# A gated mix of linear attention and a GLU: the first half's down products in seven-product form, weight sums in place, and PSUM tiles seeded from PSUM

## The chip, the cores and the metric

The kernel runs on one core of one Trainium2 chip. The metric is the device time of one execution in microseconds; the median of the runs is compared.

## The reference, cut to what matters

```python
x = A_x                                   # [1, 2048, 640], float32
g = sigmoid((x * gate_w).sum(-1, keepdims=True))
# A: linear attention, 32 heads of 20
q, k, v = heads(x @ A_wqkv)
pq, pk = phi(q), phi(k)                   # t + 1 where t > 0, else exp(t); plus 1e-6
kv, z = einsum("bhsd,bhse->bhde", pk, v), pk.sum(over s)
a = merge(einsum("bhqd,bhde->bhqe", pq, kv) / (einsum("bhqd,bhd->bhq", pq, z) + 1e-6)) @ A_wo
# B: GLU, F = 1536
b = (sigmoid(x @ B_w_gate) * (x @ B_w_up)) @ B_w_down
return g * a + (1 - g) * b
```

## The kernel before

**Numbers and products.** Every float32 operand of a matmul is split into a high half in TensorE's fp32r type and a low half that holds the rest (`split`: a ScalarE copy makes the high half, a VectorE subtraction the low one). One product is then three matmuls, high x high, high x low and low x high (`mm3`, lines 229 to 232), which accumulate in one PSUM tile. `prod` strings several products together. PSUM has eight tiles of 128 x 512, two each under the tags ch, dd, cc and rot, and `ps_tile` takes the two of a tag in turn.

**Fewer products.** Where a 2 x 2 block of weight tiles meets a 2 x 2 block of input tiles, the kernel takes Winograd's form with seven products in place of eight. It needs sums of the weight blocks (S1 to S4) and of the input blocks (T1 to T4), all split again. In the code B11, B12, B21 and B22 are the four input blocks, A11, A12, A22 weight blocks.

**Stages.** The tokens are worked in two halves of 1024 (groups 2 and 3 first, called `pr` = 1, then groups 0 and 1, `pr` = 0), each as two groups of 512 columns. First comes k and its product with x, for all tokens. Then for each half: q (`q_phase`), twelve blocks of 128 rows of F (`f_phase`), and the last down products (`last_down`). At the end the attention output is put together (`a_unit`, `ABlock`).

**One F block** has seven steps (class `Block`, `s1` to `s7`), 18 products, 54 matmuls. `s1` and `s2` are the gate's first tile of a group, in tiles ch and dd; their sum is made by a ScalarE copy of ch into an SBUF tile c11 and a VectorE add of dd. `s3`, `s5` and `s6` go on accumulating in ch, `s4` and `s7` in cc. Step 5 ends with a ScalarE copy and a VectorE add that give c22. The steps of neighbouring blocks interleave: s3, s4, s5 of block f, s1 and s2 of block f+1, then s6 and s7 of block f. Tails (`tail_f`, `tail_s`) make sigmoid(gate) x up, the h of the block, during the next block's steps 3 to 5.

**Weights.** In the first half each F block's gate and up weights come from memory as float32 (`load_w`), are split (`wg_split`, `u_part`), summed into a tile wsum (`sums`), and the sums are split into ws in two parts (`s_part`, needed at steps 3 and 5). All forms are also stored to scratch in memory, so that the second half loads them ready (`load_form`). The same is done with the down weights: `split_d` makes wd, `queue_ds` the sums and their forms ds.

**Down products.** They take h back to 640 rows and accumulate into the SBUF tile tb of 5 x 2 tiles (o = 0 to 4, groups 0 and 1). In the first half, `down_unit` makes them in the plain way: while block f runs, the pair of blocks before it gives five units of two products, for one of the two groups. In the second half `down_pair` makes both groups of a pair of blocks at once, in the seven-product form, spread over the steps of every odd block: V and W belong to o = 4, and X, Y and Z with a suffix 0 or 1 to the two column pairs o = 0, 1 and o = 2, 3. Each partial product is added into tb by VectorE (`add`), or copied by ScalarE where it is the first for its place. The last pair of each half is left to `last_down`.

**Order.** Nothing is scheduled by the compiler: instructions run on each engine in the order in which the Python code emits them. The class `Order` keeps an estimated clock for TensorE, ScalarE and VectorE (`a_cost`, `v_cost`). Side work (splits, sums, chains for the denominators) stands in queues, from urgent over items and lazy to chain and spare; `fill` emits an entry when its estimated end is at most 0.6 us (ScalarE) or 1.2 us (VectorE) past TensorE's clock, and `need(key)` emits what has not been emitted when a product is about to read it.

**Denominators.** `queue_den(g)` makes the factor of one group of 512 tokens: it loads five tiles of phi(q) again, multiplies them by z, sends the sums through memory to turn them, takes the reciprocal and sends it through memory again. Group 2's chain runs in the first half, group 3's in the q stage after it, groups 0 and 1 in the second half.

Of the kernel before, what the change touches and what calls it, by code (L numbers as in the profile page):

```python
# [29 lines left out]

class Order:

# [150 lines left out]

# [3 lines left out]

def v_cost(w):
    return 0.155 + w * 0.00104


@with_exitstack
def gated_mix_kernel(ctx: ExitStack, tc: tile.TileContext, xt, xn, wk, wv, wo, wst_q, wst_f, out_t):
# [16 lines left out]

    def ps_tile(tag):
        return psum.tile([P, 512], F32, name=tag, tag=tag, bufs=2)
# [10 lines left out]

# [35 lines left out]
    ones_f = common.tile([P, P], F32, name="ones_f")  # L274
# [19 lines left out]

# [10 lines left out]

# [6 lines left out]

# [5 lines left out]

# [8 lines left out]


# [29 lines left out]

# [10 lines left out]


# [102 lines left out]

# [28 lines left out]

# [3 lines left out]

# [48 lines left out]

# [4 lines left out]
    def queue_qw(u):  # L560
# [34 lines left out]
        for n, t in enumerate((a22, a11, a21, a12, g5)):  # L595
            piece(2, n * w, t)
# [44 lines left out]

# [71 lines left out]

# [96 lines left out]

# [28 lines left out]
    for k in range(2, KC):  # L839
        b1.k(k)  # L840
        if k == 2:
# [6 lines left out]

    nc.gpsimd.memset(logit[:, S // P:], 0.0)
    nc.gpsimd.memset(ones_f, 1.0)  # L850
    nc.gpsimd.affine_select(bd, ones_f[:bdn, :bdn].rearrange("p (b c) -> p b c", c=DH),
                            pattern=[[-DH, HPG], [0, DH]], base=0, channel_multiplier=1,
# [3 lines left out]

# [176 lines left out]

# [25 lines left out]

    entries = [("q", 1, 0)] + [("f", 1, f) for f in range(FC)]  # L1060
    WST, WS, W_AT = {}, {}, {}
# [30 lines left out]
    def queue_s(n, first=0, last=2):  # L1092

        def sums(part):
            g, u = WST[n][:, 0], WST[n][:, 1]
            if part == 0:
                WS[n] = pw2.tile([P, 9 * P], F32, name="wsum", tag="wsum")
            s = WS[n]
            c = [slice(2 * i * P, 2 * (i + 1) * P) for i in range(4)]
            if part == 0:  # L1100
                add(s[:, c[0]], u[:, c[0]], u[:, c[1]])
                sub(s[:, c[2]], g[:, c[0]], u[:, c[0]])
            else:
                sub(s[:, c[1]], s[:, c[0]], g[:, c[0]])
                sub(s[:, c[3]], g[:, c[1]], s[:, c[1]])
                sub(s[:, 8 * P:], g[:, 4 * P:], u[:, 4 * P:])
# [6 lines left out]
        cut = (0, 4 * P, 9 * P)  # L1113

        def s_part(part):
# [4 lines left out]
            split(h[:, cs], l[:, cs], WS[n][:, cs])  # L1120
# [4 lines left out]
        if first == 0:  # L1125
            order.add(0, 2 * v_cost(2 * P), lambda: sums(0), None, lambda: W_AT.get(n, 1e9))
            order.add(0, 3 * v_cost(2 * P), lambda: sums(1))
        if last > 1:
            order.add(a_cost(3 * P), v_cost(3 * P), u_part)
# [6 lines left out]
    class Block:  # L1136


        def __init__(self, n):
            self.n = n  # L1140
# [14 lines left out]
        def s1(self):  # L1155
            self.ch, self.c11 = ps_tile("ch"), c_tile("c11")
            prod(self.ch, [self.xa(0, j, j) for j in range(2)], True)
            act(self.c11, self.ch, AF.Copy, "p")

        def s2(self):  # L1160
            self.dd = ps_tile("dd")
            prod(self.dd, [self.xa(0, k, k) for k in range(2, KC)], True)
            add(self.c11, self.dd, self.c11, "p")

        def s3(self):
            self.c12 = c_tile("c12")
            prod(self.ch, self.xt(2, 2, 1), False)
            act(self.c12, self.ch, AF.Copy, "p")

        def s4(self):  # L1170
            self.cc = ps_tile("cc")
            prod(self.cc, self.xt(2, 0, 0) + [self.xb(1, 2, 4)], True)

        def s5(self):
            self.c22 = c_tile("c22")
            prod(self.ch, self.xt(2, 4, 2), False)
# [6 lines left out]
        def s7(self):  # L1183
            prod(self.cc, [self.xb(2, 6 + j, 2 + j) for j in range(2)] + [self.xb(2, 8, 4)], False)
            add(self.c12, self.cc, self.c12, "p")

# [33 lines left out]

    def gate_store():

        n = S // P
        t = tt("gates").rearrange("p (a n c) -> p a n c", n=2, c=H)
# [10 lines left out]


# [51 lines left out]

# [102 lines left out]

    down_pool, down_cms = [], []
    HT, DST, WD = {}, {}, {}
# [24 lines left out]

    def queue_ds(p):
        w, v = 4 * P, 2 * P
# [14 lines left out]
        def forms(j, h):  # L1437
            t = down_pool[1].tile([P, 2, v], F32R, name="ds", tag="ds", bufs=3)
            split(t[:, 0], t[:, 1], DST[("f", 1, 2 * p + j)][0][:, h * v:(h + 1) * v])

            def rest():
                c = 2 * D + j * w + h * v
                nc.gpsimd.dma_start(wd_dram[p][:, :, c:c + v], f32(t))
                if h:
                    load_d()
                if not (j or h):
# [907 lines left out]
```

## Time and profile before

| | |
|---|---|
| median of 3 runs | 737.26 us (737.07 to 737.29) |
| profiled execution, span from first to last instruction (the only time of it that is given) | 735.1 us |
| TensorE busy | 730.7 us, 99%, 3605 matmuls |
| VectorE busy | 554.3 us, 75%, 978 instructions |
| ScalarE busy | 334.2 us, 45%, 625 instructions |
| GpSimd busy | 97.6 us, 13%, 161 instructions |
| moved by DMA | 173.53 MB, mean 236 GB/s |

In the profile PE is TensorE's matmuls, PEld its weight loads, DVE is VectorE, ACT ScalarE, POOL GpSimd and SP the queue that issues most transfers. L230 to L232 are the three matmuls of a product, L242 any ScalarE activation, L246 any VectorE operation on two tensors, so groups are told apart by their tiles (out<-in). A time of an engine that is busy counts overlapping instructions once.

### The profile page before, as it was taken

Reading aid. Unit: us, or ns where it says so; the run is one execution under the profiler, and the core shown is the slowest. Engines: PE = TensorE matmul, PEld = TensorE weight load, DVE = VectorE, ACT = ScalarE, POOL = GpSimd, SP = SyncE. Lnnn points to the kernel's source line nnn. Section 1 sums busy time; section 2 is a strip of 40 time slices with the busy share of each in tenths; the row PEclk is TensorE's granted clock in tenths of the full one; section 3 lists DMA queues with packets and bytes.
Section 4 is the critical chain, followed back from the end, with each engine's and each line's share of the span. In section 5 each row is a group of like instructions: output and inputs, shape, how many; then the busy total and the mean of one; then the engine's idle time right before and its main releaser. Section 6 shows DMA issues by size and latency. Waiting matters only on the chain.

```text
span 735.1 us, 10117 instructions
## 1 busy us (share of the span) xinstructions
PE 730.7 (99%) x3605; PEld 628.8 (86%) x3605; DVE 554.3 (75%) x978; ACT 334.2 (45%) x625; POOL 97.6 (13%) x161
## 2 busy tenths in 40 slices
PE   9999999999999999999999999999999999999998
PEld 8999999988888888888888888888888888888886
DVE  5988877987776667877887864556778777779976
ACT  5764748268555634344444364344323222224541
POOL 0210111113312212112211211000000031000000
PEclk9999999999999999999999999999999999999999
DMA  8574648688887767666966668977778686659312
GB/s 262 134 204 99 181 115 269 162 292 304 310 319 265 290 218 274 239 237 222 365 253 224 257 206 314 352 227 249 262 264 306 253 229 242 217 200 345 113 70 100
DMA packets 70968, 173.53 MB, mean 236 GB/s; under 512 B 11610, under 2 KB 32362, under 8 KB 67206
## 3 DMA queue, kind: packets, MB, share of 16 engines
q1 hardware_dynamic: 54550, 109.99, 45.5%
q0 software_dynamic: 16224, 62.74, 24.1%
q8 instruction: 28, 0.46, 0.3%
q10 hardware_dynamic: 144, 0.16, 0.1%
q14 instruction: 22, 0.18, 0.1%
HBM read 103.96 MB, written 63.92 MB: 228 GB/s over the span
## 4 chain that ended last, share of the span: by engine, by line
PE 99%; DVE 0%; issue 0%
PE ch L230 10%; PE ch L231 10%; PE ch L232 10%; PE dd L231 8%; PE dd L230 8%; PE dd L232 8%; PE cc L232 7%; PE cc L231 7%; PE cc L230 7%; PE rot L231 6%; PE rot L232 6%; PE rot L230 6%; PE rot L1359 1%; PE rot L324 0%; PE ch L806 0%; PE dd L806 0%
## 5 line engine op out<-in xcount | busy, mean ns | idle before, releaser
L242 ACT ACTIVATE c<-ch 128x512 f32<-128x512 f32 x90 | 53.7, 597 | 184.0 <-PE ch L232 182.1
L246 DVE TENSOR_TENSOR hf<-c,hf 128x512 fp32r<-128x512 f32 x63 | 43.3, 689 | 38.8 <-ACT hf L242 38.7
L246 DVE TENSOR_TENSOR c<-cc,c 128x512 f32<-128x512 f32 x56 | 38.6, 690 | 33.8 <-ACT c L242 23.6
L246 DVE TENSOR_TENSOR tb<-dd,tb 128x512 f32<-128x512 f32 x73 | 49.7, 688 | 16.2 <-PE dd L232 16.0
L242 ACT ACTIVATE c<-c 128x512 f32<-128x512 f32 x60 | 37.8, 629 | 48.3 <-DVE c L246 47.9
L242 ACT ACTIVATE hf<-c 128x512 fp32r<-128x512 f32 x63 | 39.2, 624 | 17.1 <-DVE c L246 16.8
L246 DVE TENSOR_TENSOR tb<-rot,tb 128x512 f32<-128x512 f32 (+1 forms) x61 | 40.9, 679 | 5.2 <-PE rot L232 5.1
L230 PE MATMUL ch<-xth,ws 128*128 128x512 f32 x112 | 43.7, 390 | 0.0
L232 PE MATMUL ch<-xth,ws 128*128 128x512 f32 x112 | 43.6, 389 | 0.0
L231 PE MATMUL ch<-xtl,ws 128*128 128x512 f32 x112 | 43.6, 389 | 0.0
L230 PE MATMUL dd<-xrh,wg 128*128 128x512 f32 x90 | 35.1, 390 | 0.0
L232 PE MATMUL dd<-xrh,wg 128*128 128x512 f32 x90 | 35.0, 389 | 0.0
L231 PE MATMUL dd<-xrl,wg 128*128 128x512 f32 x90 | 35.0, 389 | 0.0
L230 PE MATMUL cc<-xbh,ws 128*128 128x512 f32 x84 | 32.7, 389 | 0.0
L231 PE MATMUL cc<-xbl,ws 128*128 128x512 f32 x84 | 32.7, 389 | 0.0
L232 PE MATMUL cc<-xbh,ws 128*128 128x512 f32 x84 | 32.7, 389 | 0.0
L231 PE MATMUL rot<-pkl,xnh 128*128 128x320 f32 x102 | 31.5, 309 | 0.0
L232 PE MATMUL rot<-pkh,xnl 128*128 128x320 f32 x102 | 31.4, 308 | 0.0
L230 PE MATMUL rot<-pkh,xnh 128*128 128x320 f32 x102 | 31.4, 308 | 0.0
L246 DVE TENSOR_TENSOR c<-c,c 128x512 f32<-128x512 f32 x44 | 30.2, 686 | 1.3 <-ACT c L242 0.9
L242 ACT ACTIVATE ws<-wsum 128x512 fp32r<-128x512 f32 (+1 forms) x26 | 17.5, 681 | 24.7 <-DVE wsum L246 24.3
L232 PEld LDWEIGHTS ch<-xth,ws 128*128 128x128 f32 x112 | 21.0, 188 | 4.4
(590 smaller groups left out, 2241.0 us busy)
## 6 DMA issues: line engine op xcount, KB each, us to landing
wf<-ws POOLq DMA_DIRECT2D x12, 1152.0 KB, 6.2
ws<-wf SPq DMA_DIRECT2D x12, 1152.0 KB, 7.6
wst<-wst_f SPq DMA_DIRECT2D x12, 640.0 KB, 5.5
wf<-wg POOLq DMA_DIRECT2D x12, 640.0 KB, 4.9
wd<-wd POOLq DMA_DIRECT2D x12, 640.0 KB, 5.8
wg<-wf SPq DMA_DIRECT2D x12, 640.0 KB, 6.0
xst<-xt SPq DMA_DIRECT2D x10, 640.0 KB, 6.8
wf<-wd SPq DMA_DIRECT2D x10, 640.0 KB, 5.6
```

The lines of the kernel that those rows point to most:

```text
L230: nc.tensor.matmul(out, l_hi, r_hi, start=first, stop=False, skip_group_check=True)
L231: nc.tensor.matmul(out, l_hi, r_lo, start=False, stop=False, skip_group_check=True)
L232: nc.tensor.matmul(out, l_lo, r_hi, start=False, stop=last, skip_group_check=True)
L242: nc.scalar.activation(out, src, fn, **kw)
L246: nc.vector.tensor_tensor(out, a, b, op=op)
L1359: nc.tensor.matmul(ps[:w, :w], v[:, m, :w], gt[:, m, c0:c0 + w], start=(m == 0), stop=(m == KC - 1))
```

## The change

Down products of the first half. `down_pair(pr, p)` now serves both halves. In the first half it reads the weights straight from wd and from ds, which is now one tile of eight column blocks, while they are also stored as before. The tails of the first half make T1 to T4 (`tail_s`), and h forms get four more buffers there. Inside `down_pair`, the first products W, X0 and X1 are no longer added into tb by themselves: ScalarE copies them into a second PSUM tile (`seed`), where V, Y0 and Y1 go on accumulating. `ps_borrow` takes the free tile of ch or cc for Y and Z1 without turning the tag. The products' order changes too: X0 and X1 with S2, Z0, then X0 and X1 with S3.

Gate. In a seeded block (all of the second half, from block 2 on in the first) step 1's result is copied by ScalarE from ch into the tile dd, and step 2 accumulates there; the sigmoid reads dd. Step 6 of block f now comes ahead of step 2 of block f+1.

Weight sums in place. The sums of a block's gate and up weights overwrite the loaded tile, after the plain splits are made; the parts of ws are laid out anew, and the second is now needed at step 4.

Moved: the denominator chains of groups 2 and 3 go to the second half, ahead of those of groups 0 and 1. The chunk of x for the second half is loaded into the tile fac, which is free until then. h forms become urgent, down weights lazy.

```diff
     def need(self, key, now=True):
-        for it in [it for it in self.urgent if it[3] == key]:
+        while (it := next((it for it in self.urgent if it[3] == key), None)) is not None:
...
+    def ps_borrow(tag):
+        slot = f"{tag}{ps_turn.get(tag, 0)}"
+        return psum.tile([P, 512], F32, name=slot, tag=slot)
+
     def ps_tile(tag):
-        return psum.tile([P, 512], F32, name=tag, tag=tag, bufs=2)
+        t = ps_borrow(tag)
+        ps_turn[tag] = 1 - ps_turn.get(tag, 0)
+        return t
...
             if part == 0:
-                WS[n] = pw2.tile([P, 9 * P], F32, name="wsum", tag="wsum")
...
+                order.need(("wg", n), False)
+                add(u[:, c[1]], u[:, c[0]], u[:, c[1]])
+                sub(u[:, c[0]], g[:, c[0]], u[:, c[0]])
             else:
+                sub(g[:, c[0]], u[:, c[1]], g[:, c[0]])
+                sub(g[:, c[1]], g[:, c[1]], g[:, c[0]])
+                sub(g[:, 4 * P:], g[:, 4 * P:], u[:, 4 * P:])
...
         def s1(self):
-            self.ch, self.c11 = ps_tile("ch"), c_tile("c11")
+            self.ch, self.dd = ps_tile("ch"), ps_tile("dd")
             prod(self.ch, [self.xa(0, j, j) for j in range(2)], True)
-            act(self.c11, self.ch, AF.Copy, "p")
+            if self.seed:
+                act(self.dd, self.ch, AF.Copy, "p")
+            else:
+                self.c11 = c_tile("c11")
+                act(self.c11, self.ch, AF.Copy, "p")
 
         def s2(self):
-            self.dd = ps_tile("dd")
-            prod(self.dd, [self.xa(0, k, k) for k in range(2, KC)], True)
-            add(self.c11, self.dd, self.c11, "p")
+            prod(self.dd, [self.xa(0, k, k) for k in range(2, KC)], not self.seed)
+            if self.seed:
+                self.c11 = c_tile("c11")
+            else:
+                add(self.c11, self.dd, self.c11, "p")
...
+        def seed(key, tag, src, borrow=False):
+            ps[key] = (ps_borrow if borrow else ps_tile)(tag)
+            act(ps[key], ps[src], AF.Copy, "p")
...
+        if pr:
+            for j in range(2):
+                order.need(("d", ("f", 1, 2 * p + j)))
+        new("W", "dd", "w0", "B11")
+        new("X0", "rot", "A11", "B11")
+        seed("V", "dd", "W")
+        new("X1", "rot", "A11", "B11", 1)
+        seed("Y1", "ch", "X1", True)
+        go("V", "w1", "B21")
+        out("V", 4, 0)
         yield
+        seed("Y0", "cc", "X0", True)
+        go("W", "w0", "T1")
+        go("W", "w1", "B22")
+        out("W", 4, 1)
+        go("Y1", "A12", "B21", q=1)
+        out("Y1", 2, 0)
+        go("Y0", "A12", "B21")
+        out("Y0", 0, 0)
+        yield
+        if pr:
+            order.need(("ds", p))
+        go("X0", "S2", "T2")
+        out("X0", 0, 1)
+        go("X1", "S2", "T2", q=1)
+        out("X1", 2, 1)
+        new("Z0", "dd", "S1", "T1")
+        out("Z0", 1, 1)
+        go("X0", "S3", "T3")
+        out("X0", 1, 1)
+        go("X1", "S3", "T3", q=1)
+        out("X1", 3, 1)
+        yield
...
-    dens = ({0: 0, 2: 1}, {4: 2})
+    dens = ({0: 2, 2: 3, 4: 0, 6: 1}, {})
...
-            elif s == 5:
+            elif s == 4:
                 order.need(("w", n, 1))
...
-            if pr:
-                if f > 1:
-                    order.need(("d", ("f", 1, f - 1 - f % 2)))
-                    for o in range(KC):
-                        down_unit(pr, f - 2 - f % 2, o, f % 2)
-                        order.fill()
...
             if f + 1 < FC:
+                step(f, 6)
                 step(f + 1, 2)
             if f in dens[pr]:
                 queue_den(dens[pr][f])
-            if f + 1 < FC:
-                step(f, 6)
             step(f, 7)
```

More of the change, by code (lines that the diff above doesn't have):

```diff
@@ L1557, in next_pools @@
         turn.update(c=4, h=0)
+    cx = []
     def c_tile(name):
[L1561 removed]
+        if "c1" in turn:
+            if not cx:
+                cx.extend(tt("cx") for _ in range(3))
+            key = "c22" if name == "c22" else "c1"
+            turn[key] += 1
+            if name == "c22":
+                return cx[turn[key] % 2]
+            if turn[key] % 6 == 0:
+                return cx[2]
+        elif "c" in turn:
             turn["c"] += 1
@@ L1661, in one @@
             order.fill()
-        def both(key, form, b, o, g, first=True):
-            at = {"A12": 0, "A22": P, "A11": D, "S2": 2 * D, "S3": 2 * D + P, "S4": 2 * D + 4 * P,
-                  "S1": 2 * D + 5 * P}[form]
-            for q in range(2):
-                one(key + str(q), [(at + 2 * q * P, b)], 2 * q + o, g, first)
-                yield
-        w0, w1 = 2 * D - P, D - P
-        seen = set()
-        x1 = both("X", "A11", "B11", 0, 0)
-        one("W", [(w0, "B11")], 4, 0)
-        next(x1)
@@ L1791, in step @@
                 order.need(("wg", n))
-                blocks[f] = Block(n)
+                blocks[f] = Block(n, not pr or f > 1)
             else:
```

216 lines of the change are left out of this document (117 added, 99 removed).

## The prediction

> **What bounds the kernel now.** I read the page first, then who waited for TensorE, then stretches of the first half's F blocks, one pair each, then single timelines. The page:
>
> ```profile
> span 735.1 us, 10117 instructions
> PE 730.7 (99%) x3605; PEld 628.8 (86%) x3605; DVE 554.3 (75%) x978; ACT 334.2 (45%) x625; POOL 97.6 (13%) x161
> PEclk9999999999999999999999999999999999999999
> PE 99%; DVE 0%; issue 0%
> ```
>
> The list of waits, for TensorE, has one row:
>
> ```profile
> PE rot L324 <- PEq L2345: 0.8, 1, 0.8
> ```
>
> So TensorE is the chain from end to end, at full clock, and its only wait is the 0.8 us at the start. A busy share proves little, because a matmul is shown longer than its slot. The timeline of TensorE says how long a slot is:
>
> ```profile
> 531.33 0.39 PE L230 MATMUL ch<-xth,ws 128*128 128x512 f32 x1
> 532.69 0.39 PE L230 MATMUL rot<-hf,wf 128*128 128x512 f32 x1
> ```
>
> Between these two starts lie six matmuls of 512 columns: 1.36 / 6 = 0.227 us each, and one product (a high and low pair, three matmuls) is 0.68 us. A matmul taken out is worth 0.227 us as long as nothing makes TensorE wait. There is no slack that hides this gain and none that hides a new wait: every stall is paid in full.
>
> **What goes.** The first half's down products, by the tile that holds their weights:
>
> ```profile
> L230 PE MATMUL dd<-hf,wd x60: 389/389/389, 216.9 to 410.7; 128*128 128x512 f32 x60
> L232 PE MATMUL rot<-hf,wd x60: 389/389/389, 218.8 to 412.6; 128*128 128x512 f32 x60
> ```
>
> These are the first and the last of six rows of 60 (two tags, three lines): 360 matmuls for six pairs of F blocks, 60 a pair, or 20 products. The seven-product form, counted in the new function, has W 3, V 1, X 8, Y 2, Z 4 = 18 products, 54 matmuls. The second half already runs that count:
>
> ```profile
> L230 PE MATMUL dd<-hf,wf x50: 389/389/389, 485.8 to 648.3; 128*128 128x512 f32 x50
> L230 PE MATMUL rot<-hf,wf x42: 283/389/389, 486.4 to 731.1; 128*128 128x512 f32 x40, 128*128 128x256 f32 x2
> ```
>
> (50 + 40 of full width in five pairs, on each of three lines: 54 a pair; the two narrow ones are of another stage.) The last pair of the first half stays as it was. So 5 pairs x 6 = 30 matmuls go: 30 x 0.227 = 6.8 us. No other matmul is added or removed: 3605 becomes 3575.
>
> **What it costs VectorE.** The first half's five pairs, one row each, and the fullest stretch of the kernel (busy us and instructions in the order PE, PEld, DVE, ACT, POOL):
>
> ```profile
> 212.20:250.30 38.10, 38.10 (x170) 31.56 (x169) 25.79 (x53) 22.50 (x44) 8.54 (x14) 1.00 0.78 287
> 250.30:288.40 38.10, 38.10 (x170) 31.56 (x169) 28.20 (x52) 14.03 (x25) 7.43 (x12) 1.00 0.68 247
> 288.40:326.40 38.00, 38.00 (x169) 31.49 (x168) 29.60 (x54) 15.02 (x28) 7.27 (x13) 1.00 0.67 234
> 326.40:364.50 38.10, 38.10 (x169) 31.54 (x168) 31.26 (x60) 15.93 (x31) 8.76 (x15) 1.00 0.83 302
> 364.50:402.60 38.10, 38.10 (x170) 31.55 (x169) 27.79 (x49) 15.33 (x28) 5.59 (x9) 1.00 0.66 237
> 664.70:704.70 40.00, 40.00 (x178) 33.13 (x177) 39.51 (x66) 17.48 (x33) 0.00 (x0) 1.00 0.54 193
> ```
>
> VectorE is busy 28.5 us a pair on the mean. What the change adds to a pair of the first half: adds into tb from 10 to 14, low halves of the h forms from 4 to 7, four sums T1 to T4; it drops the two adds of the gate (the copy goes into PSUM instead). That is +4 +3 +4 -2 = +9 operations of 512 columns. How long one holds the engine:
>
> ```profile
> L246 DVE TENSOR_TENSOR hf<-c,hf 128x512 fp32r<-128x512 f32 x63 | 43.3, 689 | 38.8 <-ACT hf L242 38.7
> L246 DVE TENSOR_TENSOR tb<-dd,tb 128x512 f32<-128x512 f32 x73 | 49.7, 688 | 16.2 <-PE dd L232 16.0
> 667.07 3.09 DVE L250 SCALAR_TENSOR_TENSOR pl<-pl,fac 128x512 f32<-128x512 f32 x5
> ```
>
> One lasts 0.69 us, yet five in a row take 3.09: (3.09 - 0.69) / 4 = 0.60 from start to start. Nine cost 5.4 us queued, 6.2 alone. The two denominator chains leave this half and the stage after it for the second half. One of them ran in these pairs, with 4 of its 5 long steps in
>
> ```profile
> L250 DVE SCALAR_TENSOR_TENSOR fac<-pden,zcol,fac x4: 742/746/748, 286.7 to 307.6; 128x512 f32<-128x512 f32 x4
> ```
>
> so at least 3.0 us in five pairs go, 0.6 a pair. New demand: 28.5 + 5.4 (or 6.2) - 0.6 = 33.3 to 34.1 us of 38.1 - 1.4 = 36.7 us a pair, 91 to 93%. That is high, but the last row of the stretches has VectorE at 39.51 of 40.00 us with TensorE at 40.00. In the second half VectorE is relieved: 17 adds a pair become 14, and all gate adds go, against the denominator chains that arrive.
>
> [...]
>
> **What it costs in waits.** Three places have a shorter distance between a product and the read or copy that must lie between it and the next one.
>
> First: X0 takes S2, is added into tb, and takes S3 after only X1 and Z0, that is three products (2.04 us) after step 5 of the block ends. Step 5's own copy and add stand ahead on VectorE. From the timeline, where step 5 ends at 532.69 (above):
>
> ```profile
> 532.95 0.60 ACT L242 ACTIVATE c<-ch 128x512 f32<-128x512 f32 x1 [8.56 <-PE ch L232]
> 533.58 0.69 DVE L246 TENSOR_TENSOR c<-cc,c 128x512 f32<-128x512 f32 x1 [1.36 <-ACT c L242]
> 534.19 0.68 DVE L246 TENSOR_TENSOR tb<-rot,tb 128x512 f32<-128x512 f32 x1
> ```
>
> The next VectorE slot is 534.19, its add ends at 534.87, 2.18 us after step 5: 0.14 late. The first pair of each half evacuates by ScalarE copies, so 8 pairs pay: 1.1 us. Bounds: 0 if VectorE gets there sooner, 0.6 more a pair (one operation ahead of it) above.
>
> Second: V is seeded by a ScalarE copy of W, due after X0 and X1. A seeded accumulation exists already (cc below, 0.59 us). ScalarE has the copy of step 3 and the split of B11 ahead:
>
> ```profile
> L242 ACT ACTIVATE cc<-tb x2: 583/590/597, 655.3 to 661.3; 128x512 f32<-128x512 f32 x2
> 522.49 0.39 PE L230 MATMUL dd<-hf,wf 128*128 128x512 f32 x1
> 522.75 0.60 ACT L242 ACTIVATE c<-ch 128x512 f32<-128x512 f32 x1 [1.96 <-PE ch L232]
> 523.24 0.62 ACT L242 ACTIVATE hf<-c 128x512 fp32r<-128x512 f32 x1
> 523.76 0.62 ACT L242 ACTIVATE c<-c 128x512 f32<-128x512 f32 x1
> 524.53 0.39 PE L230 MATMUL rot<-hf,wf 128*128 128x512 f32 x1
> ```
>
> W would start at 522.49 and V at 524.53. The third ScalarE slot, 523.76, plus 0.60 ends at 524.36, 0.17 us in time. I take 0; one more operation ahead (0.52 from start to start) makes it 0.35 late in each of 10 pairs, 3.5 us. Seeds Y0 and Y1 have a whole step more.
>
> Third: step 1 of the gate is copied into step 2's tile, and step 6 of the block before (2.04 us) now stands between them. The copy needs 0.26 + 0.60: nothing, unless ScalarE is over a microsecond behind.
>
> The denominators' chains are moved with their transfers (per chain 14 on SP, 2 on POOL, each behind the weight loads of the second half). All four now run there one behind the other, from the end of its block 0:
>
> ```profile
> L257 DVE TENSOR_SCALAR fac<-pden,zcol,zeps x2: 542/542/542, 487.8 to 564.2; 128x512 f32<-128x512 f32 x2
> L1276 POOL DMA_DIRECT2D fac_dram<-fac x4: 541/544/587, 382.0 to 618.7; - x4
> L230 PE MATMUL rot<-pq,wf x13: 283/389/389, 667.3 to 730.7; 128*128 128x512 f32 x9, 128*128 128x256 f32 x4
> ```
>
> The last chain of now runs from 564.2 to 618.7, 54.5 us. Block 0 ends two blocks of 54 matmuls (12.2 us each) and a step (1.4) ahead of the first down product (485.8, above): 460. Four chains end at 460 + 218 = 678. The last factor is first asked for after five units of five products in the attention stage, about 667 + 17 = 684. In time, so nothing, by some 6 us.
>
> The rest at nothing. Sums in place have the same sizes and drop a tile; the forced gate split ahead of them is work that comes anyway. The down weights' sums are split in two of 512 columns instead of four of 256, and stored in as many transfers of the same bytes; they are lazy, with most of a pair to go in. All of it lies under TensorE's slots; if that cover went, it would show as the second or last rival.
>
> **The sum.** 735.1 - 6.8 + 1.1 = 729.4 us of span. The median, 737.26, stands 2.2 us above the profiled span, so 731.6 us. Two tenths of a per cent, 1.5 us, is what a measurement here can tell.
>
> **Rivals.**
> *Seeds late.* ScalarE gets one more split ahead of V's seed in every pair. For it: the fill rule may put one there, and a split that waits for VectorE holds all behind it. Against: 45% busy. 731.6 + 3.5 = 735.1 us. Chance 0.13, and mostly still faster.
>
> *VectorE becomes the bound.* If each operation costs its full duration, the 54 a pair of now (mean of the five rows) lose up to 0.09 each of overlap, 4.8 us: 28.5 + 4.8 + 6.2 - 0.6 = 38.9 against 36.7 us. Over four pairs (the first has copies in place of 10 adds) that takes back 8.8 us: 735.1 - 6.8 + 8.8 + 2.2 = 739.3. The spacing of 0.60 us and the full stretch at 664.7 bear against it. Chance 0.07. [...]
>
> *The denominators come too late.* If the fourth chain runs over, its last stages are forced onto VectorE in the full stretch, each behind a round trip through memory. What that may cost I bound by the gap between two stages, 54.5 us over some 5 waits for memory, 11 us: 742.6. Chance 0.04: the margin is thin, but VectorE has less to do there than now.
>
> *The weights come too late (slower).* The order written by the kernel counts 0.155 + 512 x 0.00104 = 0.687 us for each such operation, so it may see the 38.9 us of the rival above in 36.7, an engine that is full, and find no room for the weights' halves. What finds no room is emitted by force at the step that reads it, and the second half of the sums is now read in step 4, not 5. There TensorE waits for the add ahead and the low half:
>
> ```profile
> L246 DVE TENSOR_TENSOR ws<-wsum,ws 128x512 fp32r<-128x512 f32 (+1 forms) x26 | 19.6, 754 | 6.4 <-ACT ws L242 6.3
> ```
>
> 0.26 (product to ScalarE, above) + 0.69 + 0.75 = 1.7 us each. It decides from the fourth such piece on (three take 5.1 of the 5.7 us left); one in each of ten blocks gives 731.6 + 17 = 748.6. For it: 91 to 93% leaves little, and after each pair the h forms crowd into one block of 12.2 us. Against: the next block is twice as long, and lazy work can give way. Chance 0.14, of which 0.05 is three or fewer, faster or level.
>
> **The numbers.** Forecast 0.62, own range 730.5 (no wait) to 733.5. Faster: 0.62 + 0.10 (seeds) + 0.02 (few pieces) = 0.74. Same: 0.03 + 0.03 (VectorE) + 0.03 = 0.09. Slower: 0.04 (VectorE) + 0.04 (denominators) + 0.09 = 0.17. The range is 730.3 to 736.7: the lower end is the sum without any wait, less 0.2 for the spread of the runs; the upper takes in late seeds and three forced pieces (731.6 + 5.1); above it lie VectorE as the bound, late denominators and many forced pieces, 0.20.
>
> **What would show it.** Right: 3575 matmuls, a span near 729.4, at most 0.2 us of wait at X0's second use, VectorE at 33 to 34 us a pair in the first half. Wrong: gaps ahead of V behind ScalarE (first rival), VectorE with no idle time through several pairs and TensorE waiting for adds (second), gaps in the attention stage behind fac (third), gaps at steps 3 and 4 that end with a low half of ws (fourth).

## The result: 804.35 us, 9% slower, and the profile after

The changed kernel takes 804.35 us (median of four runs, 800.65 to 808.18) against 737.27 us beside it: 1.0906 times the kernel before, 95% interval 1.0863 to 1.095. The forecast was 731.6 us. The page of the profiled execution, the slowest of the four:

```profile
span 806.0 us, 10081 instructions
PE 750.3 (93%) x3575; PEld 628.8 (78%) x3575; DVE 568.2 (71%) x987; ACT 357.8 (44%) x661; POOL 94.6 (12%) x161
PEclk9999999998999999999999999999999899999589
PE 64%; DVE 11%; DMA 10%; issue 9%; ACT 4%; SPq 1%; POOL 1%; DVEq 0%; POOLq 0%; ACTq 0%
```

The 3575 matmuls are there, but TensorE is 64% of the chain that ended last where it was 99%, and it did not always have its full clock (0.972 granted on the mean). The largest waits of TensorE (us in total, times, longest):

```profile
PE dd L214 <- ACT dd L225: 13.8, 8, 3.7
PE dd L214 <- DVE dd L229: 11.5, 1, 11.5
PE cc L214 <- ACT pq L225: 4.5, 1, 4.5
PE ch L214 <- DMA ws<-wf: 3.9, 1, 3.9
PE cc L214 <- ACT ws L225: 3.8, 5, 1.2
PE ch L214 <- ACT c L225: 3.1, 1, 3.1
```

By place these are the gate seed (row 1), the last denominator chain (2, 3), a load of the second half (4), the second piece of ws (5), and the first half's q stage (6). In the rest of this text, lost time is what the starts of TensorE's matmuls lie further apart than at full pace (0.227 us for 512 columns), added up from all of them. In the profiled execution, by stage:

| stage, us of the profile | lost us |
|---|---|
| q stage, 141 to 206 | 9.7 |
| first half's F blocks, 206 to 425 | 26.6 |
| their last down products, 425 to 520 | 3.4 |
| second half, 520 to 730 | 5.3 |
| attention stage, from 730 | 20.0 |
| 61 matmuls at half clock (0.50 granted), 0.20 each | 12.2 |

The sum is 77.2 us; 806.0 less the forecast span of 729.4 is 76.6. Four pairs of F blocks of the first half, from one down pair's first product to the next one's (columns as in the prediction's stretches):

```profile
241.70:284.00 42.30, 38.26 (x164) 30.07 (x163) 31.33 (x58) 25.96 (x46) 9.07 (x17) 1.00 0.65 249
284.00:324.10 40.10, 37.94 (x164) 30.02 (x163) 31.42 (x56) 15.72 (x28) 4.49 (x8) 1.00 0.48 177
324.10:365.70 41.60, 38.44 (x164) 29.98 (x163) 32.67 (x56) 17.84 (x32) 6.79 (x12) 1.00 0.56 212
365.70:412.20 46.50, 40.04 (x164) 31.10 (x163) 36.56 (x65) 18.70 (x33) 6.80 (x12) 0.96 0.65 241
sum 170.50, PE 154.67 PEld 121.18 DVE 131.97 ACT 78.22 POOL 27.15; mean PE 38.67 PEld 30.29 DVE 32.99 ACT 19.55 POOL 6.79
```

A pair should take 36.7 us and takes 42.6. VectorE has 33.0 us of work in it, close to the forecast, and does nothing for the other 9.6 us. The experiments are about that contradiction.

### The profile page after: what moved, and what is told of

It reads as the page before. It is cut to its first block, busy times and chain, and to the rows that moved or that the text cites. A ratio compares the mean times of both kernels' runs of the same rounds, so it can differ in the third digit from the quotient of the medians.

```text
span 806.0 us, 10081 instructions
## 1 busy us (share of the span) xinstructions
PE 750.3 (93%) x3575; PEld 628.8 (78%) x3575; DVE 568.2 (71%) x987; ACT 357.8 (44%) x661; POOL 94.6 (12%) x161
## 4 chain that ended last, share of the span: by engine, by line
PE 64%; DVE 11%; DMA 10%; issue 9%; ACT 4%; SPq 1%; POOL 1%; DVEq 0%; POOLq 0%; ACTq 0%
PE ch L214 6%; PE ch L216 6%; PE ch L215 6%; PE cc L216 6%; PE cc L215 5%; PE cc L214 5%; PE dd L214 5%; PE dd L216 5%; PE dd L215 5%; PE rot L214 4%; PE rot L215 4%; PE rot L216 4%; DMA ws<-wf 2%; DVE tb L229 1%; DVE hf L229 1%
## 5 line engine op out<-in xcount | busy, mean ns | idle before, releaser
L229 DVE TENSOR_TENSOR hf<-c,hf 128x512 fp32r<-128x512 f32 x74 | 50.7, 689 | 48.9 <-ACT hf L225 47.8
L225 ACT ACTIVATE c<-ch 128x512 f32<-128x512 f32 x50 | 29.8, 595 | 98.6 <-PE ch L216 98.5
L225 ACT ACTIVATE hf<-c 128x512 fp32r<-128x512 f32 x74 | 46.0, 626 | 48.5 <-DVE c L229 48.2
L214 PE MATMUL ch<-xth,ws 128*128 128x512 f32 x112 | 44.8, 400 | 7.0 <-DMA ws<-wf 3.9
L229 DVE TENSOR_TENSOR c<-cc,c 128x512 f32<-128x512 f32 x38 | 26.2, 690 | 35.2 <-PE cc L216 18.5
L214 PE MATMUL dd<-xrh,wg 128*128 128x512 f32 x90 | 36.3, 403 | 12.6 <-ACT dd L225 12.6
L216 PE MATMUL ch<-xth,ws 128*128 128x512 f32 x112 | 44.6, 398 | 0.0
L229 DVE TENSOR_TENSOR tb<-rot,tb 128x512 f32<-128x512 f32 (+1 forms) x59 | 38.2, 676 | 6.3 <-PE rot L216 5.4
L229 DVE TENSOR_TENSOR tb<-dd,tb 128x512 f32<-128x512 f32 x44 | 30.2, 687 | 13.4 <-PE dd L216 13.3
L216 PE MATMUL dd<-xrh,wg 128*128 128x512 f32 x90 | 35.9, 399 | 0.0
L215 PE MATMUL cc<-xbl,ws 128*128 128x512 f32 x84 | 33.3, 396 | 0.0
L214 PEld LDWEIGHTS dd<-xrh,wg 128*128 128x128 f32 x90 | 17.1, 190 | 18.5 <-ACT dd L225 15.1
L225 ACT ACTIVATE ws<-wst 128x640 fp32r<-128x640 f32 (+1 forms) x26 | 17.4, 679 | 30.7 <-DVE wst L229 17.9
L214 PEld LDWEIGHTS ch<-xth,ws 128*128 128x128 f32 x112 | 21.4, 191 | 12.2 <-DMA ws<-wf 4.3
```

Of the source, the lines that this page charges most:

```text
L214: nc.tensor.matmul(out, l_hi, r_hi, start=first, stop=False, skip_group_check=True)
L215: nc.tensor.matmul(out, l_hi, r_lo, start=False, stop=False, skip_group_check=True)
L216: nc.tensor.matmul(out, l_lo, r_hi, start=False, stop=last, skip_group_check=True)
L225: nc.scalar.activation(out, src, fn, **kw)
L229: nc.vector.tensor_tensor(out, a, b, op=op)
```

## The experiments

**1. The gate seed first.** The timeline of after shows how a gate seed comes late:

```profile
357.36 1.99 DVE L229 TENSOR_TENSOR wst<-wst 128x256 f32<-128x256 f32 x5
359.44 0.74 ACT L225 ACTIVATE ws<-wst 128x640 fp32r<-128x640 f32 x1 [3.40 <-issue]
360.08 0.58 ACT L225 ACTIVATE dd<-ch 128x512 f32<-128x512 f32 x1
360.71 0.50 PE L214 MATMUL dd<-xrh,wg 128*128 128x512 f32 x1 [2.43 <-ACT dd L225]
```

The split of ws on ScalarE starts 0.09 us after VectorE's five sums end (357.36 + 1.99 = 359.35; the row puts its idle time down to "issue"). The seed (dd<-ch) is issued behind that split and comes after it. The edit issues the seed first:

```diff
-            if pr and s == 1:
-                order.need(("w", n, 0), False)
...
             getattr(blk, f"s{s}")()
+            if pr and s == 1:
+                order.need(("w", n, 0), False)
```

> Edit: in the first half, step 1 of a block issues ScalarE's gate seed before the weights' first ws piece is forced, and not behind it. Theory (the seed stands in ScalarE's order behind a split that waits for VectorE's in-place sums): the eight waits of TensorE for the gate seed in the first half, 13.7 us in the profile of after, go almost all; time 804 -> 788 to 797 us. Rival (VectorE itself has too much to do in the first half, the order does not matter): the wait moves to steps 3 and 4 of the same blocks, TensorE's waits in the first half stay at 25 us or more; 801 us or above.

Measured: 804.01 us (1.0906, 1.0872 to 1.0941), no gain. TensorE's waits in the first half's blocks:

```profile
PE cc L214 <- ACT ws L225: 5.4, 5, 1.8
PE cc L214 <- DVE tb L229: 4.2, 1, 4.2
PE rot L214 <- DVE tb L229: 2.8, 1, 2.8
PE dd L214 <- ACT dd L225: 1.8, 3, 1.1
```

The seed's 13.8 us are 1.8, and ws and tb have taken their place: 26.1 us lost there instead of 26.6. Time and waits lie where the rival put them (801 us or above, 25 us or more): the order decided where the time showed, but changing it gained none.

**2. No gate seed.** The seed is a copy on ScalarE that saves VectorE an addition; here the additions come back.

```diff
-                blocks[f] = Block(n, not pr or f > 1)
+                blocks[f] = Block(n, not pr)
```

> Edit: no block of the first half has a gate seed; VectorE adds the first product to the second as in before (eight more additions of about 0.69 us, 5.5 us of VectorE in the first half). Theory (the seed's place in ScalarE's order costs 13.7 us): the waits for it go, some come back because VectorE has less room; 792 to 799 us. Rival (VectorE is the bound of the first half): slower than after, 806 us or more.

Measured: 815.54 us (1.1056, 1.1023 to 1.109), 11 us slower than after and in the rival's range; 34.4 us lost in the blocks, 8 more than in run 1. VectorE has ten additions more there (6.8 us, not 5.5). But a single wait of TensorE makes 11.7 of the 34.4 us, and behind it ScalarE waits for the load of a down weight (us, times, longest):

```profile
ACT wd L225 <- DMA dst<-wst_f: 13.3, 3, 10.7
```

The first theory (the seed's place) fell with these two runs. That VectorE has no room was the new one; because of that one wait, this run alone does not show it.

**3. Denominators two at a time.**

```diff
-    dens = ({0: 2, 2: 3, 4: 0, 6: 1}, {})
+    dens = ({0: (2, 3), 4: (0, 1)}, {})
...
+        k = KC + 1
+        seq = [i for two in zip(x[:k], y[:k]) for i in two]
+        seq += [x[k], x[k + 1], y[k], x[k + 2], y[k + 1], y[k + 2]]
```

In after, the four chains' first operation starts between these times, and VectorE sits idle (us, times, longest) for the fourth one's transfers from 725 to 765 us:

```profile
L240 DVE TENSOR_SCALAR fac<-pden,zcol,zeps x4: 540/541/542, 507.1 to 731.5; 128x512 f32<-128x512 f32 x4
DVE fac L233 <- DMA pden<-p_dram: 9.5, 3, 3.9
DVE hf L233 <- DMA fac<-fac_dram: 7.0, 2, 5.0
DVE fac L229 <- DMA fac<-den_dram: 6.3, 1, 6.3
```

> Edit: the denominators' chains run two at a time (groups 2 and 3 from the first block of the second half, 0 and 1 from the fifth), operations of the two by turns; the first half is as in after. Theory (the fourth chain ends after it is asked for, and TensorE's waits for it also halve its clock): the 20 us of waits in the attention stage fall under 4, and the half-speed records between 744 and 772 us go; 804 -> 770 to 782 us. Rival 1 (the half clock has nothing to do with the waits): the waits go and the slow records stay in the last 60 us; about 786. Rival 2 (VectorE has no room for the chains earlier): the waits move into the second half, 795 or above.

Measured: 778.75 us (1.0559, 1.0516 to 1.0602). The same row, and the attention stage as one stretch:

```profile
L240 DVE TENSOR_SCALAR fac<-pden,zcol,zeps x4: 539/540/542, 507.8 to 585.8; 128x512 f32<-128x512 f32 x4
700.00:778.00 78.00, 78.00 (x359) 65.03 (x357) 65.59 (x110) 31.54 (x59) 0.00 (x0) 1.00 0.51 185
```

The last chain starts at 585.8 and not at 731.5, no time is lost in the attention stage, and its clock is 1.00 throughout: 25.6 us. That the late chains cost this is shown.

> Edit: both of the former, the seed issued first and the denominators two at a time. Theory: the gains add up, since the one lies in the first half and the other behind it: 804 - 13 - 28 = 763 us, 755 to 772. Rival (the time that one gives is taken by the other): within 5 us of the better of the two alone.

Runs 1 and 3 together: 777.29 us (1.0528, 1.0511 to 1.0545), so again nothing for the seed. This version is the base of the next three.

**4. Less work, or no tie?** In after a split of ws waits for sums made in place, a tie that the kernel before had only to a tile of its own. Either the tie or the amount of work can make VectorE late. One run leaves the sums out (no work, no tie), one keeps the work and cuts the tie, one hands the sums to GpSimd:

```diff
-                add(u[:, c[1]], u[:, c[0]], u[:, c[1]])
-                sub(u[:, c[0]], g[:, c[0]], u[:, c[0]])
...
+                add(g[:, c[1]], u[:, c[0]], u[:, c[1]])
+                sub(g[:, c[0]], g[:, c[0]], u[:, c[0]])
...
-            split(h[:, cs], l[:, cs], WST[n][:, part, :cut[part + 1] - cut[part]])
+            split(h[:, cs], l[:, cs], WST[n][:, 1, :cut[part + 1] - cut[part]])
```

(the diff of the second; the first only drops the five operations, the third replaces them by GpSimd's.)

> Edit on the version with the seed first and the denominators two at a time (777.3 us, 26.5 us of TensorE's waits in the first half's blocks): the weights' sums are left out, so that ws holds split copies of the raw gate and up weights; 50 additions and subtractions of 0.28 to 0.42 us, some 20 us of VectorE, are not done, and no split waits for them. Theory V (VectorE has too much work in the first half, 88% of TensorE's own time, and the waits come from that): the waits there fall under 8 us; 752 to 762 us. Rival D (the in-place sums make ScalarE's splits wait for VectorE, and that order is the cause): the same fall; it is told apart by the next run.

> Edit on the same version: the sums are done, as many and as long, but all into the gate half of the staging tile after it has been split, and both ws splits read the raw up weights (so ws holds no sums): VectorE's work is kept and no split waits for a sum. Theory V: the waits in the first half's blocks stay at 20 us or more; 771 to 780 us. Rival D: they fall under 10 us; 762 us or less.

> Edit on the same version: the weights' five sums a block run on GpSimd instead of VectorE, nothing is left out. VectorE is relieved of 20 us as in the run without sums, and the splits wait for GpSimd. Theory V: most of the gain of the run without sums, 752 to 768 us, if GpSimd takes no more than some 5 us a block. Rival D: the sums come later than VectorE's did, and it is slower than 777 us.

Measured: 769.56 us, 774.20 us and 790.42 us (1.0433, 1.0499 and 1.072). Lost in the first half's blocks: 16.0, 23.7 and 22.8 us, where the base has 26.5. So the tie alone is worth some 3 us at most (the times of that run and of the base overlap), but leaving the sums out did not give what theory V asked for (under 8). Three single events make up 14.6 us of the 16.0, and at each ScalarE has a down weight's split at the head of its order that waits for its load (us, times, longest, in the run without sums):

```profile
ACT wd L225 <- DMA dst<-wst_f: 25.1, 3, 10.3
```

With the sums on GpSimd the kernel is slower than the base, as theory D had it: ScalarE's splits wait for GpSimd's sums, and VectorE itself is slowed (0.95 us instead of 0.69 for one kind of addition, last section). The run with the sums on GpSimd:

```profile
ACT ws L225 <- POOL wst L255: 22.7, 8, 5.5
```

**5. Sums and seeds alone.** The kernel before with only the sums in place and the first half's gate seeds; and the same with the seed issued first, the second piece of ws after step 2 and the value weights' loads first. The diff of the first:

```diff
-                blocks[f] = Block(n)
+                blocks[f] = Block(n, pr and f > 1)
...
-            elif s == 5:
+            elif s == 4:
                 order.need(("w", n, 1))
```

> Edit on the kernel before: only the weights' sums in place (with their layout and step 4's earlier need of them) and the gate's first product seeded in the first half's blocks from the third on; the first half's down products stay in plain form, the denominators where they were. VectorE has 5.5 us less to do there than in the kernel before (76% of TensorE's time). Theory V: no wait of the first half of the size of after's, within 3 us of the kernel before, 735 to 740 us. Rival D: 10 us or more slower than the kernel before, most of the 26 us.

> The kernel before with the sums in place and the gate seeds (754.7 us), now with the seed issued first, the second piece of ws after step 2, and the value weights' loads first. Theory O: the ten waits for the seed (11.3 us) and the 3 us for the value weights go: 738 to 743 us. Rival (in-place sums or seeds cost it in any order): 750 us or more.

Measured: 754.67 us (1.0232, 1.0215 to 1.0249) and 751.72 us (1.0193, 1.0178 to 1.0208); theory D of the first run (10 us or more slower) and the rival of the second (750 us or more) had these numbers, but not the cause. The waits of the two:

```profile
PE dd L230 <- ACT dd L242: 8.6, 10, 1.7
```

```profile
PE dd L230 <- ACT dd L242: 7.3, 10, 1.2
```

There step 2 follows step 1 directly, and ten times TensorE stands while ScalarE copies its product (0.8 us or more, 10 of the 14 us lost, in the second run). So these runs say little of after, which has step 6 between the two; what they show is the price of such a seed with nothing between. Nothing else keeps TensorE waiting in these blocks of theirs, where VectorE has some 29 us of work in the 40 us of a pair: there the sums in place cost no time.

**6. Five orders.** On the base: (a) value weights' loads first on SP's queue, (b) cx tiles only after the q stage, (c) ws's second piece after step 2, (d) 9 us planned for a down weight's load, (e) denominators' loads on GpSimd's queue.

```diff
(a)  load_mv(0); load_mv(1); load_w(); load_mv(2)
(b)  next(q, None), and only then turn.update(c1=0, c22=0, h=0)
(c)  +  if pr and s < 3: order.need(("w", n, s - 1), False)
(d)  -  DST[n] = (t, order.pe + 4.0)
     +  DST[n] = (t, order.pe + 9.0)
(e)  nc.sync.dma_start(...) -> nc.gpsimd.dma_start(...) in load, turn_in, turn_out
```

> Five orders mended on the version with the seed first and the denominators two at a time (777.3 us): (a) the first two loads of the value weights go to SP's queue ahead of the first staged weights, which wait for their place; (b) the three tiles cx are taken from the pool of the feature map's tiles only after the q stage; (c) the second piece of ws is forced right after step 2, not at step 4; (d) a down weight's load is taken to need 9 us, not 4, before its split is put in ScalarE's order; (e) the denominators' loads go through GpSimd's queue, not SP's. Theory O (the waits left are those of single orders: an instruction that waits stands ahead of one that TensorE needs): q stage 7.7 -> 3 us, first half's blocks 26.5 -> 12 us, second half 4.9 -> 1.2 us, 7 us of half clock -> 2; 748 us, 742 to 757. Theory V (VectorE's work as a whole): only (a), (b) and (e) give something, first half's blocks stay over 22 us; 765 us.

> The five orders without (c): the second piece of ws is again forced only at step 4. Theory O: step 4's waits for ws (11 us in the version with seed first and pairs) stay, 7 to 11 us slower than with all five. If ws's second piece is not what costs: within 2 us of all five.

> The five orders without (d): a down weight's split is again put 4 us behind its load in the plan. Theory O: ScalarE waits some 13 us in the first half for loads of down weights, and the three or four events of TensorE behind them (some 8 us) come back: 5 to 10 us slower than with all five. If not: within 2 us.

Measured: 764.12 us (1.0347, 1.0317 to 1.0377), 763.92 without (c), 769.43 without (d). Together they give 13 us, not 29: the time is theory V's, and the blocks' 19.2 us lie between theory O's 12 and theory V's 22. (d) is worth 5, as theory O had it, (c) nothing: step 4's waits (8.4 us without it) are replaced by waits of the down pair's seed and splits. The blocks lose 19.2 and 18.9 us with and without it.

Two more runs put the down pair's seeds and ds splits ahead of what the planner lets in before them:

```diff
+            was, order.busy = order.busy, True
             act(ps[key], ps[src], AF.Copy, "p")
+            order.busy = was
...
+            if pr: order.need(("ds", p), False)      # now at the end of the second part
```

> On the version with the five orders (764.1 us; 19.2 us of TensorE's waits in the first half's blocks, of them 17.7 for the down pair's seed V and its ds splits, 6.2 us in the second half): (f) the planner puts nothing in ScalarE's order right ahead of a down pair's seed, and V's comes right after W; (g) the ds splits are forced before step 5 and not behind its copy; (h) the loads of the gathered output matrix's rows go through GpSimd's queue too; (i) the second block's gate weights are forced one step earlier. Theory O (single orders): the first half's waits fall to 4 to 8 us, the second half's to 1.2; 748 us, 744 to 753. Theory V (no room on VectorE): the waits move to ws, wg or the forms and stay over 15 us in the first half's blocks; 758 us or more.

> The same without (c), so that the second piece of ws is again forced only at step 4. Theory O: step 4's waits for ws (8 to 9 us with the five orders less (c)) come on top of the former run: 754 to 760 us. Theory V: no difference over 2 us between the two.

Measured: 772.70 and 765.05 us (1.0484 and 1.0378). The first loses 24.5 us in the blocks, more than before the edit, now for wd and wg; the second 18.4. Whatever is put first, something else is late, as theory V had it for the first run. But it had no difference between the two, and they lie 7.6 us apart: the order counts as well.

**7. The amount of work, in steps.** On the five orders: all the sums of ws left out, the tie alone cut, and only the down weights' sums left out.

> The version with the five orders (764.1 us, 19.2 us of TensorE's waits in the first half's blocks) without the weights' sums, so that ws holds split copies of raw weights: 20 us of VectorE less. Theory V (the first half's blocks leave VectorE too little room): the waits there fall to 5 us or less; 748 us, 745 to 752. If they were single orders with nothing to do with the amount: 12 us or more stay.

> The same version with the sums done but all into the gate half of the staging tile, and ws split from the raw up weights: VectorE's work is kept, no split waits for a sum. Theory V: 15 to 21 us of waits stay in the first half's blocks; 760 to 766 us. Theory D (the tie between sums and splits): 8 us or less; 753 us or less.

> The same version without the down weights' sums (20 operations of 0.42 us, 8.4 us of VectorE), so that ds holds split copies of raw down weights; the gate and up weights' sums are in place as in after. Theory V: two fifths of what the run without the other sums gains, 757 us, 754 to 760. Theory D: no change, 762 us or more.

Measured: 743.73 us (1.0086, 1.0061 to 1.011), 758.69 (1.0299) and 753.68 (1.0239). The sums over four pairs of the first half, for the five orders (with the first and the last pair), then without the down weights' sums, then without those of ws:

```profile
230.40:270.90 40.50, 37.66 (x164) 30.20 (x163) 30.50 (x57) 24.44 (x43) 8.02 (x15) 1.00 0.69 243
351.50:391.80 40.30, 37.87 (x164) 30.05 (x163) 34.59 (x61) 17.82 (x32) 7.13 (x13) 1.00 0.70 252
sum 161.40, PE 151.00 PEld 120.56 DVE 131.69 ACT 77.62 POOL 27.08; mean PE 37.75 PEld 30.14 DVE 32.92 ACT 19.40 POOL 6.77
```

```profile
sum 155.50, PE 150.31 PEld 120.74 DVE 124.25 ACT 76.97 POOL 26.35; mean PE 37.58 PEld 30.19 DVE 31.06 ACT 19.24 POOL 6.59
```

```profile
sum 148.30, PE 148.30 PEld 121.11 DVE 116.78 ACT 78.13 POOL 26.03; mean PE 37.08 PEld 30.28 DVE 29.19 ACT 19.53 POOL 6.51
```

A pair takes 40.4, 38.9 and 37.1 us while VectorE has 32.9, 31.1 and 29.2 us of work in it: what VectorE does not use is 7.4, 7.8 and 7.9 us on the mean. That is no fixed loss: single pairs leave from 5.7 us (the last one of the five orders) to 10.9, and 37.1 us is so close to TensorE's own 36.7 that the third figure says little of VectorE. The blocks lose 19.2, 12.3 and 1.3 us. With the tie cut and the work kept, 16.7 us stay, so of the 17.9 us that the first run gains there at most 2.5 are the tie's. The three times lie 0.3 to 1.3 us below theory V's ranges; the waits of the first two runs are within them.

Without the five orders, leaving out the same sums kept 16.0 us (run 4). So of the base's 26.5 us less work alone (with the tie gone) took 10.5, better order alone 7.3, and both together 25.2: with these orders the amount of VectorE's work sets the pace, but neither is enough alone. Whether the run without the down weights' sums gains by the work or by ds's splits, which no longer wait for a sum, it does not tell.

**8. The same amount in the kernel before.**

```diff
+            if pr and s in (2, 4, 7):
+                order.add(0, v_cost(IW), lambda: add(idle, idle, idle))
```

> The kernel before with three additions of 512 columns more in every block of the first half (36 in all, on a tile of their own that nobody reads), put into the planner's list like the weights' work: VectorE gets some 21 us more in the first half's blocks and comes to 86% of TensorE's time there, as in the version with the five orders (87%). Theory V (the amount of VectorE's work): TensorE gets waits of 8 to 20 us in the first half's blocks; 745 to 758 us. Rival (only the change's own ties make the work late): under 2 us of waits, 740 us or less.

Measured: 758.69 us (1.0276, 1.0244 to 1.0309), 0.7 us above theory V's range. The first half's blocks lose 12.4 us, within its range, where the kernel before lost none. The stretch from its first pair to 425 us:

```profile
212.20:425.00 212.80, 203.00 (x868) 164.91 (x867) 169.28 (x305) 85.83 (x161) 39.74 (x66) 0.98 0.69 247
```

VectorE leaves 43.5 us unused, in 5.3 pairs of 40.4 us (38.1 + 12.4 / 5.3): 8.3 a pair on the mean. Here too a single stretch leaves less: from 288.4 to 328.1 us VectorE has 35.6 us of work in 39.7. The additions cost more than the blocks' 12.4 us: another 4.6 are lost in the second half, where TensorE waits for a load of ws, and some 7 to matmuls at half clock. Thirty-six additions that nothing reads slow this kernel by 21 us, without one product, seed or sum of the change.

No run beats the kernel before. The one without the sums of ws, which leaves them undone, is still 6 us behind it.

## Why the prediction was wrong, step by step

- **TensorE's products** (6.8 us to gain): right. 3575 matmuls, 54 a pair.
- **VectorE's room**: this step failed. Its demand was nearly right (33.3 to 34.1 us a pair forecast, 33.0 measured). It was set against 36.7 us, all of TensorE's time, as if VectorE never stood still. In after 33.0 us of work took a pair of 42.6 us; with the five orders 32.9 took 40.4; only at 29.2 did the pair come near 36.7. Much of VectorE's unused time goes in waits for ScalarE, whose half of every split must come first. After's list of VectorE's waits from 206 to 425 us begins with them, and these four rows make 39.3 of the 53.3 us that it does not use there:

```profile
DVE hf L229 <- ACT hf L225: 20.6, 14, 3.6
DVE ws L229 <- ACT ws L225: 8.1, 9, 1.2
DVE cx L229 <- ACT cx L225: 6.1, 8, 1.3
DVE wd L229 <- ACT wd L225: 4.5, 4, 2.1
```

  The stretch at 664.7 us, with VectorE at 39.51 of 40.00 us, was taken as proof that it can be full. It was full there, in the attention stage; in no pair of the first half's blocks was it. The mean pair of the kernel before had 28.5 us of VectorE in it and the fullest 31.3 of 38.1, with no wait of TensorE; 36 additions more brought them (run 8). Spacing against duration, weighed there, was not the question.
- **The rival of VectorE as the bound** (0.07) named the engine, but another mechanism: each operation at its full duration, and VectorE with no idle time through several pairs. Here it stands unused for 9.6 us of a pair. It put 8.8 us on four pairs; measured are 170.5 - 146.8 = 23.7, some 1.6 of them at half clock.
- **X0's second use**: right in kind, and in its sum by luck. In the second half four pairs lose 0.24 us each (two matmuls late) and the fifth 0.14, 1.1 us in all; forecast were 0.14 in each of eight pairs of both halves, 1.1 in all.
- **V's seed**: in time in the second half, late in the first (six matmuls, 2.0 us).
- **The gate seed** ("nothing, unless ScalarE is over a microsecond behind"): it was. 13.8 us; the condition was named and given no chance.
- **Weights at step 4**: late in five blocks (15 matmuls), 6.0 us or 1.2 a block. The rival's place was right; it had ten blocks at 1.7 us.
- **Denominators** (in time by 6 us): wrong, and its own row said so. The 54.5 us run from the last chain's first operation to its last store. Between the first operations of the two chains in that row lie 564.2 - 487.8 = 76.4 us, since a chain's loads start only when the one before is done (in before the last chain's first loads are issued at 551.98 us, behind the other's last at 550.18). Here the first operations of the four are (731.5 - 507.1) / 3 = 74.8 us apart. The rival (0.04) put 11 us on it; 20.0 us are lost and clock besides, 25.6 us by run 3.
- **The q stage** had no step: 9.7 us. Some 2 of them are a wait for value weights. Without the tile of the sums the first staged weights lie elsewhere, and their load waits, presumably for that place, at the head of SP's queue with the value weights behind it (before, then after):

```profile
132.94 0.33 SPq L1074 DMA_DIRECT2D wst<-wst_q  x1
133.32 9.29 SPq L1303 DMA_DIRECT2D wv_sb<-wv  x3
```

```profile
141.92 0.33 SPq L1035 DMA_DIRECT2D wst<-wst_q  x1
142.30 1.56 SPq L1262 DMA_DIRECT2D wv_sb<-wv  x3
```

  The rest are mainly waits for ScalarE's copies and splits, the longest 3.1 us (after's waits, row 6).
- **The clock** had no step either: 12.2 us.
- The four rivals were given separate chances. The waits that they named came all at once, three of them in the same blocks, where one took the place of another as the order changed.

What stays open: how VectorE's unused time of a pair divides between ScalarE's lead, the costs by which the planner places the work (no run changed them) and the loads; and 4.5 us in the q stage and 5.0 in the second half (1.0 of them X0's) that the five orders left even without the sums.

## What to carry to other kernels

An engine that alternates with another one in order can have less room than the time that TensorE takes (VectorE left 9.6 us of a pair unused in after, 7.4 with the five orders): take its usable share from stretches with the same kind of work, and treat demand above what they hold as a risk, however much of its time seems free. When several waits move on as each is mended, take work away from one engine in two sizes, in the old order and in the new: that tells what the amount is worth and what the order. A chain of round trips through memory is to be timed by the period it will have in its new place (74.8 us here, not 54.5), and two such chains can run in each other's gaps (the last one began at 585.8 us instead of 731.5).

## What the runs showed of the hardware

**The granted clock fell to 0.50 behind some waits of TensorE.** After the wait of 2.43 us at 235.19, TensorE's matmuls start 0.42 us apart, then 0.23 again; the fifth and sixth rows are stretches, with the granted clock in the third column from the end:

```profile
238.67 0.63 PE L215 MATMUL cc<-xbl,ws 128*128 128x512 f32 x1
239.09 0.63 PE L216 MATMUL cc<-xbh,ws 128*128 128x512 f32 x1
240.32 0.39 PE L214 MATMUL cc<-xbh,ws 128*128 128x512 f32 x1
240.55 0.39 PE L215 MATMUL cc<-xbl,ws 128*128 128x512 f32 x1
235.80:239.00 3.20, 3.20 (x10) 2.54 (x9) 0.31 (x1) 0.46 (x1) 0.00 (x0) 0.58 0.28 82
744.40:758.00 13.60, 3.88 (x9) 3.11 (x10) 3.21 (x6) 0.00 (x0) 1.08 (x2) 0.52 0.20 63
```

From 236.4 to 239.7 us the granted clock is 0.50. The records of the slow clock within the span last 3.41, 6.83, 10.24 or 13.65 us. A wait of the same 2.43 us, the one at 360.71 in experiment 1, left the clock at 1.00. The slow records of this profile begin at 195.4, 236.3, 407.0, 635.7, 744.9 and 762.0 us, whole multiples of 3.41 us apart, so the span can be cut into steps of that length. The first wait lies in one step, 232.9 to 236.3, of which matmuls at full pace fill 0.30; the second lies across two, filled 0.68 and 0.52. In the whole profile the full-clock steps just before the six falls are filled 0.07 to 0.36; those that stay at full clock are filled 0.46 or more, but for one of 0.35 at 144 us. Ten waits of at most 1.2 us, 7.3 together (second run of 5), left the clock at 1.00 from 212.2 to 425 us. Whether a step's fill is what brings the fall, these runs do not show.

**Beside GpSimd's sums VectorE was slower.** With the sums on GpSimd, two of VectorE's rows in the first half's blocks, of after and of that run:

```profile
L229 DVE TENSOR_TENSOR tb<-rot,tb 128x512 f32<-128x512 f32 x21 | 13.6, 683 | 1.8 <-PE rot L216 1.5
L229 DVE TENSOR_TENSOR c<-cx,c 128x512 f32<-128x512 f32 x13 | 8.9, 685 | 0.1
```

```profile
L229 DVE TENSOR_TENSOR tb<-rot,tb 128x512 f32<-128x512 f32 x19 | 12.2, 681 | 1.0 <-PE rot L216 0.6
L229 DVE TENSOR_TENSOR c<-cx,c 128x512 f32<-128x512 f32 x13 | 12.4, 953 | 1.3 <-ACT c L225 1.2
```

The addition with both inputs in SBUF takes 0.95 us on the mean instead of 0.69, the one with an input in PSUM is unchanged at 0.68. The four sums cx<-cx of two SBUF tiles take 1.22 us on the mean, in after 0.69; hf<-c,hf (32) 0.85 and c<-c,c (12) 0.83, in after 0.69 both. One by one, the 28 operations of 512 columns on two SBUF inputs that overlap a sum on GpSimd take 1.05 to 1.22 us (the means by tile), those beside no such sum 0.68 to 0.69; the eight with an input in PSUM that overlap one take 0.67 to 0.69.
